# Moving one more chunk's first expert layer to seven block products, and reordering VectorE's work around it

## Chip, cores, metric

One core of a Trainium2 chip (trn2). The metric is the device time of one execution in microseconds (us), the median of several runs. "Span" is the time from the first to the last instruction of the profiled execution; it is 1.7 to 2.1 us shorter than the device time. Runs in a state with a lower granted TensorE clock are marked slow and left out of all comparisons.

## What is computed

The reference, cut to what matters:

```python
# attention: B=4 batches, H=8 heads, S=768, D=64; k and v are mixed over 8 blocks by a
# doubly normalised matrix P (5 rounds of exp and normalising), then attention within blocks
k_sorted = einsum('bhij,bhjcd->bhicd', P, k_blocks)      # v_sorted likewise
attn = softmax(q_block @ k_sorted_block.T / sqrt(D))
x = (attn @ v_sorted_block) -> [3072 tokens, 512]
# expert layer: 4 experts, 512 -> 1024 -> 512
p = domain_probs / (domain_probs.sum(-1) + 1e-9)
for e in range(4):
    h = maximum(x @ w1[e], 0)
    out += p[:, e:e+1] * (h @ w2[e])
```

Almost all matrix work is in the two expert layers, 3072 x 512 x 1024 x 4 twice. The kernel multiplies 2 x 2 blocks of matrices with seven block products instead of eight, at the price of sums of blocks before and after. The second layer does so for all experts at once in nearly all chunks; the first layer only in some.

## The kernel before

The tokens go through in twelve chunks of 256, three to a batch; I number them 0 to 11. While TensorE works on the chunks of batch *b*, the attention of batch *b+1* is laid between its products at numbered "slots" by a plan of entries (chunk, slot, function, batch, pair):

```python
PLANS = {0: [ ...
    (2, 2, st_lk, 2, 1), (2, 2, st_bk, 2, 1), (2, 3, st_a, 1, 2),      # st_bk: pattern for the K mix
    (2, 4, st_x, 1, 2), (2, 4, st_q, 2, 0), (2, 5, st_s, 1, 3),
    (2, 5, st_q, 2, 1), (2, 6, st_v, 2, 0), (2, 7, st_a, 1, 3), ...    # st_v: V mix, st_s: scores, st_a: attention
```

First layer with all products (chunks 0 to 5): 32 matmuls of 256 columns to an expert, each half evacuated by VectorE (taken out of its PSUM bank, with relu and weighting, and written to `Hb`), then sums of blocks of the result for the second layer:

```python
def chunk_first(b, c, es, first, slot):
    for e in es:
        for g in range(2):
            # 4 x 4 matmuls into two PSUM banks ... (cut)
            nc.vector.scalar_tensor_tensor(out=Hb[:, e, ...], in0=ps[:], scalar=0.0, op0=ALU.max,
                                           in1=pb[...], op1=ALU.mult)
            if e > first:
                for w in ((1,), (2,) if b or c else (2, 3))[g]:
                    h_sums(e - 1, w)
            slot()
```

First layer with seven products (chunks 6 to 11): 7 x 8 matmuls of 128 columns to an expert. Products 1, 6, 7, 4 run through one bank X (1 is made in Z and copied), 5 and 3 through a bank Q; ScalarE copies between them and VectorE finishes the quarters:

```python
def p1(): product(Z, "a11", "b11", True); nc.scalar.copy(X, Z)
def p5(): product(Q, "s1", "t1", True)
def p6(): product(X, "s2", "t2");         nc.scalar.copy(u2, X)
def p2(): product(Z, "a12", "b21");       finish(0, 0, Z)
def p7(): product(X, "s3", "t3");         nc.scalar.copy(u3, X); tt(t22, Q, u3, ALU.add)
def p4(): product(X, "a22", "t4");        finish(1, 0, X)
def p3(): product(Q, "s4", "b22");        tt(t12, Q, u2, ALU.add)
```

It needs four sums of weight blocks to an expert (s1 to s4, 128 x 1024 each). Before the change VectorE makes all sixteen, nearly all of them during chunk 5. The results of matmuls go to eight PSUM banks: the kernel uses four for chunk and second layer (psM), four for attention (psA). Attention is over in chunk 5, and `last_banks` hands first psA, later psM to the seven-product scheme.

The softmax here doesn't subtract the row's maximum and nothing guards it: scores larger than these inputs give would overflow.

Of the kernel before, what the change touches and what calls it, by code (L numbers as in the profile page):

```python
# [17 lines left out]
def kernel(  # L18
# [411 lines left out]
    def st_a(b, pr):  # L430
        if b == B - 1 and pr >= H // 2 - 2:
            xsl = arena[:, ds((pr + 2) * NB * 2 * D, NB * 2 * D)].rearrange("p (i h d) -> p i h d", i=NB, h=2)[0:BLK]
        else:
            xsl = att.tile([P, NB, 2, D], F16, name=f"xsl_{b}_{pr}", tag="xsl")[0:BLK]
        xsls[(b, pr)] = xsl
        vs = vss[(b, pr // 2)]
        for hh in range(2):
            ET = ETs[2 * (pr % 2) + hh]
            ps = psa([P, 2, 512], F32, f"ps_a_{b}_{pr}_{hh}")
            for i in range(NB):  # L440
                nc.tensor.matmul(  # L441
                    ps[:, i // HB, ds((i % HB) * VW, D + 1)],
                    ET[:, ds(i * BLK, P)],
                    vs[:, i, 2 * (pr % 2) + hh, 0:D + 1],
                    start=True, stop=True,
                )
            normalize(ps, xsl, hh)
# [153 lines left out]
    def st_bk(b, qd):  # L601
# [6 lines left out]
            (0, 9, st_v, 1, 0), (0, 10, st_q, 1, 0), (0, 10, st_v, 1, 1), (0, 11, st_k, 1, 0), (0, 11, st_n, 1, 1),  # L608
# [6 lines left out]
            (2, 1, st_n, 2, 2), (2, 1, st_n, 2, 3), (2, 2, st_lk, 2, 1), (2, 2, st_bk, 2, 1), (2, 3, st_a, 1, 2),  # L615
            (2, 4, st_x, 1, 2), (2, 4, st_q, 2, 0), (2, 5, st_s, 1, 3),
            (2, 5, st_q, 2, 1), (2, 6, st_v, 2, 0), (2, 7, st_a, 1, 3), (2, 8, st_x, 1, 3), (2, 8, st_v, 2, 1),
# [3 lines left out]
            (0, 0, st_k, 2, 1), (0, 1, st_lk, 3, 0), (0, 1, st_n, 3, 1), (0, 2, st_a, 2, 0), (0, 2, st_q, 2, 3),  # L621
# [112 lines left out]
    def h_sums(e, which):  # L734
        blk = lambda kh, tok: Hb[:, e, ds(kh * KH, KH), ds(tok * P, P)]
        sm = [Sb[:, n, e].rearrange("p (f x) -> p f x", f=KH) for n in range(4)]
        tt = nc.vector.tensor_tensor
        if which == 1:
            tt(sm[0], blk(0, 1), blk(1, 1), ALU.add)  # L739
        elif which == 2:  # L740
            tt(sm[1], sm[0], blk(0, 0), ALU.subtract)
        elif which == 3:
            tt(sm[2], blk(0, 0), blk(0, 1), ALU.subtract)
        else:
            tt(sm[3], blk(1, 0), sm[1], ALU.subtract)
# [13 lines left out]
    def chunk_first(b, c, es, first, slot):  # L759

        xT = xTs[b].rearrange("p k i x -> p k (i x)")
        pb = pbs[(b, c)]
        for e in es:
            for g in range(2):
                ps = psm([P, 4, 2 * P], F32, f"ps_h_{b}_{c}_{e}_{g}")
                for f in range(4):
                    for kc in range(NKC):
                        nc.tensor.matmul(  # L768
                            ps[:, f, :],
                            w1sb[e][:, kc, ds((4 * g + f) * P, P)],  # L770
                            xT[:, kc, ds(2 * c * P, 2 * P)],
                            start=(kc == 0), stop=(kc == NKC - 1),
                        )
                nc.vector.scalar_tensor_tensor(  # L774
                    out=Hb[:, e, ds(4 * g, 4), :], in0=ps[:], scalar=0.0,
                    op0=ALU.max, in1=pb[:, ds(e, 1), :].broadcast_to([P, 4, 2 * P]), op1=ALU.mult,
                )
                if e > first:
                    for w in ((1,), (2,) if b or c else (2, 3))[g]:
                        h_sums(e - 1, w)  # L780
                slot()

    def chunk(b, c, slot, done=()):
# [5 lines left out]
        for w in range(1, 3 if b else 1 + c if c else 3):  # L789
            h_sums(E - 1, w)  # L790
# [6 lines left out]
        def product(n, lhs, rhs, pool=psm):  # L797
            ps = pool([P, DH], F32, f"ps_{n}_{b}_{c}")
            for e in es:
                if pool is last_bank and e == 2:  # L800
                    last["e0"][6]()
# [19 lines left out]
        if b or c:  # L821
            two = [psm([P, 2, 512], F32, f"ps_p{n}_{b}_{c}") for n in range(2)]
            bankA, bankB, bankC, bankQ = [two[n // 2][:, n % 2, 0:DH] for n in range(4)]
            if last:
                bankQ = last["Q"][1][:, 0:DH]
        if b:
# [9 lines left out]
            for e in es:  # L836
                h_sums(e, 3)
# [3 lines left out]
            for e in es:  # L841
                h_sums(e, 4)
# [3 lines left out]
            times(bankA, sm(2), "t3", es, False)  # L846
# [4 lines left out]
            times(bankQ, sm(3), "b22", es, False, True, last["e0"][6] if last else None, 2 if last else None)  # L851
# [4 lines left out]
        if c:  # L856
# [7 lines left out]
            for w in range(1 + c, 3):  # L864
                h_sums(E - 1, w)
# [81 lines left out]
    def a_block(n):  # L947
        return arena[:, ds(n * AW, AW)].rearrange("p (k f) -> p k f", k=2)


    A_ORDER = (6, 7, 8, 0, 1, 2, 3, 4, 5, 9, 10, 11)
    As = []
    for e in range(E):
# [4 lines left out]
            "s1": a_block(A_ORDER[3 * e]), "s3": a_block(A_ORDER[3 * e + 1]), "s2": a_block(A_ORDER[3 * e + 2]),  # L958
        })

    def input_sums(e, n, half=None):
        a = As[e]
        dst, x, y, op = (
            ("s1", "a21", "a22", ALU.add), ("s3", "a11", "a21", ALU.subtract),
            ("s2", "s1", "a11", ALU.subtract), ("s4", "a12", "s2", ALU.subtract),
        )[n]
        part = slice(None) if half is None else slice(half, half + 1)
        nc.vector.tensor_tensor(a[dst][:, part], a[x][:, part], a[y][:, part], op)
# [3 lines left out]
    G0 = 2 * (R // 2)  # L972
    GN = B * (R // 2)

    def token_sums(g):
# [7 lines left out]
            "t1": t3[:, 0], "t2": t3[:, 1], "t3": t3[:, 2],  # L983
            "t4": wide[g % 2][:, 0:2 * P].rearrange("p (k x) -> p k x", k=2),
        }
        for dst, x, y in (("t1", "b12", "b11"), ("t2", "b22", "t1"), ("t3", "b22", "b12"), ("t4", "b21", "t2")):
            nc.vector.tensor_tensor(t[dst], t[x], t[y], ALU.subtract)
# [14 lines left out]
    def prepare_last():  # L1002

        last_banks(0)
        last["n"] = 1
        t = moe.tile([P, NKC, NB, BLK], F16, name="tmp7", tag="xT").rearrange("p k i x -> p (k i x)").bitcast(F32)
        room = [t[:, ds(n * 512, 512)] for n in range(3)]
        for m in range(2):
            t = att.tile([P, NB, 4, VW], F16, name=f"tmp7_{m}", tag="vs").rearrange("p i h w -> p (i h w)")
            t = t[:, 0:2048].bitcast(F32)  # L1010
            room += [t[:, 0:512], t[:, 512:1024]]
        t = att.tile([P, NB, 2, D], F16, name="tmp7_2", tag="xsl").rearrange("p i h d -> p (i h d)").bitcast(F32)
        room.append(t)
        for n, nm in enumerate(("u2", "u3", "t22", "t12")):
            last[nm] = room[2 * n:2 * n + 2]

    def last_bank(shape, dtype, name):
        n = last["n"]
        last["n"] += 1
        return last["Q"][2 - n % 2][:, 0:shape[1]]  # L1020

    def seven(g, e):

        a, t, pb = As[e], Bs[g], pbs[divmod(g, R // 2)]
        X, Z, u2, u3, t22, t12 = [last[nm][e % 2] for nm in ("X", "Z", "u2", "u3", "t22", "t12")]
        X, Z, Q = X[:], Z[:], last["Q"][e][:]
# [30 lines left out]
        def p6():  # L1057
            product(X, "s2", "t2")
# [29 lines left out]
    def last_chunk(g):  # L1088
        b, c = divmod(g, R // 2)
        final = g == GN - 1  # L1090
        last["e0"][2]()
        if g == G0:
            last_banks(1)
        prs = [last["e0"]] + [seven(g, e) for e in range(1, E)]
        for e in range(1, E):
# [3 lines left out]
            if e > 1:  # L1099
                prs[e - 2][12]()  # L1100
            now[5]()
# [5 lines left out]
            for n in late_sums.pop((g, e), ()):  # L1107
                input_sums(*n)
# [5 lines left out]
        bankB, bankA, bankC, bankQ = [t[:, 0:DH] for t in last["Q"]]  # L1114
# [35 lines left out]
        for e in range(E):  # L1150
            h_sums(e, 4)
# [4 lines left out]
        for e in range(E):  # L1156
            h_sums(e, 3)
        product(bankQ, sm(3), "b22", False, range(2))
        if not final:
            token_sums(g + 1)  # L1160
        product(bankA, sm(2), "t3", False)
        if not final:
            last_begin(g + 1)
# [3 lines left out]
        product(bankQ, sm(3), "b22", False, range(2, E), None if final else last["e0"][6], 3)  # L1167
# [8 lines left out]
        (1, 11, 0, 0), (1, 13, 0, 1), (2, 1, 0, 2), (2, 3, 1, 0), (2, 5, 1, 1), (2, 7, 1, 2),  # L1176
        (2, 8, 2, 0), (2, 9, 2, 1), (2, 10, 2, 2), (2, 10, 0, 3), (2, 11, 1, 3), (2, 11, 3, 0), (2, 12, 2, 3),
        (2, 13, 3, 1), (2, 14, 3, 2),
    ]
    late_sums = {(G0, 1): [(3, 3, 0)], (G0, 2): [(3, 3, 1)]}  # L1180
# [112 lines left out]
    for b in range(2):  # L1293
        for c in range(R // 2):
            done = (1, 2) if (b, c) == (0, 0) else ()
            at = [2 * len(done)]

            def slot(b=b, c=c, at=at):
                here = (c, at[0])
                for cc, n, f, *args in PLANS[b]:  # L1300
                    if (cc, n) == here:
                        f(*args)
                if b:
                    for cc, n, e, m in PLAN_A:
                        if (cc, n) == here:
                            input_sums(e, m)
                    if here == (R // 2 - 1, 7):
                        prepare_last()
                    if here == (R // 2 - 1, 12):
                        token_sums(G0)  # L1310
                    if here == (R // 2 - 1, 13):
                        last_begin(G0)
                at[0] += 1

            chunk(b, c, slot, done)
    for g in range(G0, GN):
# [29 lines left out]
```

## Time and profile before

| | before |
|---|---|
| device time, median of 6 runs | 365.28 us (364.46 to 365.92) |
| span of the profiled run | 362.5 us, clock 1.000 |
| chunk 1, 2, 3, 4 (start to start of TensorE's first product) | 23.05, 24.64, 32.20, 32.94 us |
| chunk 5 (to expert 0's second product of chunk 6, both dummy matmuls counted in) | 28.02 us |
| chunks 7 to 11 | 24.7 us each |

The busy time by engine, from the page of the kernel before (us, share of the span, instructions; PEld is the loading of weights, beside PE):

```profile
PE 354.1 (98%) x4517; PEld 314.6 (87%) x4517; DVE 280.0 (77%) x559; ACT 157.7 (44%) x282; POOL 117.5 (32%) x134
```

How to read what follows. In TensorE's order of time each line is a group of matmuls: start, printed length, source line, output<-inputs, shape, count. Printed lengths run into the next group, so lengths are taken from start to start. "Landing" is the time from the issue of a transfer to its arrival. A bracket at the end of a line names how long the engine was idle before it and what released it. Source lines differ by a few between kernels: L1032 before is L1038 after, L1121 is L1141.

### The profile page before, as it was taken

How to read it: one execution, taken by the hardware profiler on the slowest of the kernel's cores; microseconds unless marked ns; L12 is line 12 of the kernel's file. 1: busy time of each engine (PE TensorE's matmuls, PEld its weight loads, DVE VectorE, ACT ScalarE, POOL GpSimd, SP SyncE). 2: the span in 40 equal slices, each digit the busy share in tenths (PEclk: the TensorE clock that was granted, in tenths of full speed). 3: DMA queues.
4: the chain of work that ended last, by engine and by line, in shares of the span. 5: the costliest groups of instructions: out<-in, count | busy, mean ns of one | idle time of the engine just before them, and what ended most of it. 6: DMA issues, size and time to landing. Idle time of an engine off the chain costs nothing.

```text
span 362.5 us, 10556 instructions
## 1 busy us (share of the span) xinstructions
PE 354.1 (98%) x4517; PEld 314.6 (87%) x4517; DVE 280.0 (77%) x559; ACT 157.7 (44%) x282; POOL 117.5 (32%) x134
## 2 busy tenths in 40 slices
PE   8799999999999999999999999999999999999996
PEld 8685857888888888988888899999999998999995
DVE  5753898779798676866799979868779679587794
ACT  2664430452424355367400157165283381561740
POOL 8882011655022420000000018137055082180470
PEclk9999999999999999999999999999999999999999
DMA  8999999999999999934450310310301101102101
GB/s 109 206 208 230 208 210 200 194 186 158 175 197 162 210 91 172 161 85 73 85 126 2 58 60 4 58 60 4 88 31 49 71 2 60 61 2 65 55 16 44
DMA packets 69753, 38.34 MB, mean 106 GB/s; under 512 B 40390, under 2 KB 64716, under 8 KB 69708
## 3 DMA queue, kind: packets, MB, share of 16 engines
q0 software_dynamic: 34640, 17.83, 38.5%
q1 hardware_dynamic: 35068, 19.85, 27.0%
q8 instruction: 35, 0.57, 0.6%
q14 instruction: 10, 0.08, 0.1%
HBM read 42.00 MB, written 6.34 MB: 133 GB/s over the span
## 4 chain that ended last, share of the span: by engine, by line
PE 86%; DVE 6%; DMA 5%; issue 1%; ACT 1%; POOL 1%; DVEq 0%; ACTq 0%
PE ps_Q L1121 20%; PE ps_h L768 18%; PE ps_p L753 13%; PE ps_X L1032 9%; PE ps_Z L1032 6%; PE ps_Q L1032 6%; DMA w<-in_moe_w_dram 4%; PE ps_o L696 3%; PE ps_p L803 2%; PE ps_h L661 1%; PE ps_s L406 1%; PE ps_a L441 1%; PE ps_k L387 1%; DVE Hb L774 1%; PE ps_v L354 1%
## 5 line engine op out<-in xcount | busy, mean ns | idle before, releaser
L1045 POOL TENSOR_TENSOR Hb<-tmp,pb 128x512 f16<-128x512 f32 x48 | 62.0, 1297 | 150.5 <-ACT tmp L1044 148.7
L768 PE MATMUL ps_h<-xT,w 128*128 128x256 f16 x672 | 78.4, 273 | 0.0
L768 PEld LDWEIGHTS <-w 128*128 128x128 f16 x672 | 64.5, 98 | 8.5
L774 DVE SCALAR_TENSOR_TENSOR Hb<-ps_h,pb 128x1024 f16<-128x1024 f32 x42 | 51.3, 1223 | 17.6 <-PE ps_h L768 17.4
L1032 PEld LDWEIGHTS <-w 128*128 128x128 f16 x768 | 46.6, 98 | 0.8
L1121 PEld LDWEIGHTS <-Sb 128*128 128x128 f16 x384 | 37.2, 98 | 4.1
L1032 PEld LDWEIGHTS <-arena 128*128 128x128 f16 x576 | 34.7, 98 | 0.1
L1044 ACT ACTIVATE tmp<-tmp 128x512 f32<-128x512 f32 x48 | 30.5, 635 | 6.4 <-DVE tmp L1076 5.2
L753 PEld LDWEIGHTS <-Sb 128*128 128x128 f16 x288 | 27.4, 98 | 4.2 <-issue 0.7
L1121 PEld LDWEIGHTS <-Hb 128*128 128x128 f16 x288 | 27.4, 98 | 2.9
L413 ACT ACTIVATE ET<-ps_s 96x768 f16<-96x768 f32 x24 | 18.1, 802 | 26.1 <-PE ps_s L406 25.8
L1032 PE MATMUL ps_X<-kT,arena 128*128 128x128 f16 x384 | 29.3, 219 | 0.0
L121 POOL DMA_DIRECT2D arena<-in_q_dram x24 | 19.9, 837 | 27.1 <-DMA qT<-arena 17.2
L396 ACT CAST kT<-ps_k 64x384 f16<-64x384 f32 x48 | 22.7, 473 | 13.2 <-PE ps_k L387 12.2
L739 DVE TENSOR_TENSOR Sb<-Hb 128x512 f16<-128x512 f16 x45 | 26.5, 609 | 0.0
L1068 DVE TENSOR_TENSOR tmp<-ps_Q,tmp 128x512 f32<-128x512 f32 x24 | 16.6, 691 | 12.2 <-ACT tmp L1067 8.0
L1121 PE MATMUL ps_Q<-w,Sb 128*128 128x256 f16 x192 | 24.7, 273 | 0.0
L1121 PE MATMUL ps_Q<-w,Hb 128*128 128x256 f16 x192 | 23.9, 273 | 0.0
L1052 ACT COPY ps_X<-ps_Z 128x512 f32<-128x512 f32 x24 | 13.7, 570 | 22.8 <-PE ps_Z L1032 22.4
L753 PEld LDWEIGHTS <-Hb 128*128 128x128 f16 x216 | 20.6, 98 | 3.1 <-issue 0.3
L1121 PE MATMUL ps_Q<-T,Sb 128*128 128x256 f16 x192 | 22.9, 273 | 0.0
L1059 ACT COPY tmp<-ps_X 128x512 f32<-128x512 f32 x24 | 14.1, 586 | 12.2 <-PE ps_X L1032 12.2
(189 smaller groups left out, 605.3 us busy)
## 6 DMA issues: line engine op xcount, KB each, us to landing
w<-in_moe_w_dram POOLq DMA_DIRECT2D x7, 1024.0 KB, 27.0
pb<-p_dram SPq DMA_DIRECT2D x12, 512.0 KB, 5.5
arena<-in_k_dram POOLq DMA_DIRECT2D x8, 384.0 KB, 8.6
arena<-in_v_dram POOLq DMA_DIRECT2D x8, 384.0 KB, 9.6
vs<-arena SPq DMA_DIRECT2D x36, 66.0 KB, 5.2
arena<-in_q_dram POOLq DMA_DIRECT2D x24, 96.0 KB, 6.7
out_dram<-ob SPq DMA_DIRECT2D x9, 256.0 KB, 2.0
out_dram<-oa SPq DMA_DIRECT2D x8, 256.0 KB, 2.4
```

Source lines behind the costliest of these rows:

```text
L121: nc.gpsimd.dma_start(t[:, h // 2, :, h % 2, :], q[b, h].rearrange("(t p) d -> p t d", p=P))
L396: nc.scalar.copy(kT[ds(D * hh, D), r], pk[ds(D * r, D), hh].rearrange("p a (i c) -> p a i c", c=CP),)
L413: nc.scalar.activation(ETs[2 * (pr % 2) + hh][:, 0:S].rearrange("c (a x) -> c a x", a=2), pss[hh][0:BLK, :, 0:HS], AF.Exp, bias=0.0, scale ...
L739: tt(sm[0], blk(0, 1), blk(1, 1), ALU.add)
L753: nc.tensor.matmul(ps, lhs(e, f), Ts[e][rhs][:, f, :], start=(first and e == es[0] and f == 0), stop=(done and e == es[-1] and f == KH - 1 ...
L768: nc.tensor.matmul(ps[:, f, :], w1sb[e][:, kc, ds((4 * g + f) * P, P)], xT[:, kc, ds(2 * c * P, 2 * P)], start=(kc == 0), stop=(kc == NKC ...
L774: nc.vector.scalar_tensor_tensor(out=Hb[:, e, ds(4 * g, 4), :], in0=ps[:], scalar=0.0, op0=ALU.max, in1=pb[:, ds(e, 1), :].broadcast_to([P ...
L1032: nc.tensor.matmul(dst[:, ds(f * P, P)], a[lhs][:, k, ds(f * P, P)], t[rhs][:, k, :], start=(first and f == 0 and k == 0), stop=(f == KH - ...
L1044: nc.scalar.activation(src, src, AF.Relu, bias=0.0, scale=1.0)
L1045: nc.gpsimd.tensor_tensor(Hb[:, e, ds(i * KH, KH), ds(j * P, P)], src.rearrange("p (f x) -> p f x", f=KH), pb[:, ds(e, 1), ds(j * P, P)].b ...
L1068: tt(t22, Q, u3, ALU.add)
L1121: nc.tensor.matmul(ps, lhs(e, f), Ts[e][rhs][:, f, :], start=(first and e == 0 and f == 0), stop=(e == E - 1 and f == KH - 1), skip_group_ ...
```

## The change

Its intent: chunk 5 takes the cheaper first layer for experts 1 to 3 (expert 0 keeps all products and fills the time of the changeover). For that the weight sums must be ready earlier. Expert 1's stay on VectorE, those of experts 2 and 3 become a scaling on ScalarE and an accumulating transfer issued by GpSimd, expert 0's come during chunk 5. Two block sums of the result are written in place, which frees a quarter of `Sb` twice for other tiles. Around it VectorE's order is changed: the K pattern goes a chunk later, block sums go behind both evacuations ("late"), output adds ahead of one block sum.

```diff
         0: [
-            (2, 1, st_n, 2, 2), ..., (2, 2, st_lk, 2, 1), (2, 2, st_bk, 2, 1), (2, 3, st_a, 1, 2),
+            (2, 1, st_n, 2, 2), ..., (2, 2, st_lk, 2, 1), (2, 3, st_a, 1, 2),
-            (2, 5, st_q, 2, 1), (2, 6, st_v, 2, 0), (2, 7, st_a, 1, 3), (2, 8, st_x, 1, 3), ...
+            (2, 5, st_q, 2, 1), (2, 6, st_a, 1, 3), (2, 7, st_v, 2, 0), (2, 8, st_x, 1, 3), ...
         1: [
-            (0, 0, st_k, 2, 1), (0, 1, st_lk, 3, 0), ...
+            (0, 0, st_k, 2, 1), (0, 0, st_bk, 2, 1), (0, 1, st_lk, 3, 0), ...
@@ chunk_first
-                if e > first:
-                    for w in ((1,), (2,) if b or c else (2, 3))[g]:
+                late = e == E - 1 or b > c
+                if e > first and (g or not late):
+                    two = (2,) if b or c else (2, 3)
+                    for w in (1, *two) if late else ((1,), two)[g]:
                         h_sums(e - 1, w)
@@ chunk: the last expert's second block sum, chunk 2
-        for w in range(1, 3 if b else 1 + c if c else 3):
+        for w in range(1, 2 if c and not b else 3):
             h_sums(E - 1, w)
             ...
             tt(oa1, bankB, oa1, ALU.add)
-            for w in range(1 + c, 3):
-                h_sums(E - 1, w)
+            h_sums(E - 1, 2)
@@ input_sums
+        if vector:
+            nc.vector.tensor_tensor(a[dst], a[y], a[x], ALU.add if sign > 0 else ALU.subtract)
+        else:
+            nc.scalar.mul(a[dst], a[x], sign)
+            nc.gpsimd.dma_start(a[dst], a[y], accum_op=ALU.add)
@@ last_chunk (lead: chunk 5)
+        if lead:
+            chunk_first(b, c, [0], 0, slot)
+            last_banks(0)
+            last_tmp(g)
+            prs = {1: seven(g, 1)}
+            prs[1][1]()
+            prs[1][5]()
+            seven(g, 2)[5]()
+            prs[1][2]()
+            prs[1][6]()
+            input_sums(0, 0, True)
+            input_sums(0, 1, True)
+            last_banks(1)
@@
     PLAN_A = [
+        (1, 8, 1, 0, True), (1, 8, 1, 1, True), (1, 8, 1, 2, True), (1, 10, 1, 3, True),
+        (1, 8, 2, 0), (1, 8, 2, 1), (1, 9, 3, 0), (1, 10, 3, 1), (1, 11, 2, 2), (1, 12, 3, 2), (1, 13, 2, 3),
+        (2, 0, 3, 3),
     ]
   (cut: in-place block sums, homes of tiles, signs of sums, temporaries, the loop over chunks,
    an earlier query transpose at (0, 7))
```

## The prediction

> **What bounds the kernel now.** I read the clock and the 40-slice table first, then the chain of work that ended last, then TensorE's own order of time beside VectorE's, chunk by chunk. A chunk is 256 tokens: a first expert layer with relu and weighting, then a second layer as one matrix product with seven block products. There are twelve, three to a batch; I number them 0 to 11.
>
> The 40-slice table:
>
> ```profile
> PE   8799999999999999999999999999999999999996
> DVE  5753898779798676866799979868779679587794
> PEclk9999999999999999999999999999999999999999
> ```
>
> The clock is full throughout and TensorE is 90% busy or more from the fourth slice on. Busy TensorE is not TensorE without waits, so the next thing to read is where its groups start. The chain, around the chunk that the change rewrites (chunk 5) and in a later chunk:
>
> ```profile
> 183.82 14.03 PE ps_h L768 x128
> 198.07 3.49 PE ps_p L753 x32
> 201.56 1.75 PE ps_Q L753 x16
> ...
> 238.99 0.89 PE ps_X L1032 x16
> ```
>
> From these come two rates. Wide matmuls (256 columns, L768 and L753) take 1.75/16 = 109 ns each, narrow ones (128 columns, L1032) 0.89/16 = 55.6 ns. I use 109.1 and 55.6. A later chunk has 4 experts x 56 narrow and 112 wide: 12.46 + 12.22 = 24.7 us. The busy table by stretch shows that such a chunk really takes that:
>
> ```profile
> 183.66:212.13 28.47, 28.47 (x280) 25.46 (x277) 26.57 (x51) 2.65 (x6) 0.00 (x0) 1.00 0.27 57
> 236.88:261.60 24.72, 24.72 (x339) 23.45 (x337) 19.42 (x41) 12.74 (x25) 10.32 (x8) 1.00 0.18 45
> ```
>
> (Columns: stretch, its length, then busy PE, weight load, DVE, ACT, POOL.) So from chunk 6 to the tail nothing but TensorE's own work counts, and in chunk 5 too: 240 wide at 109.1 ns, 32 narrow at 55.6 and two dummy matmuls give 28.4 of its 28.47 us. There only removed matmuls pay.
>
> Chunks 1 to 4 also carry the attention of the next batches, and there TensorE waits in places. TensorE's order of time in chunk 2:
>
> ```profile
> 102.24 3.66 PE L768 MATMUL ps_h<-xT,w 128*128 128x256 f16 x32
> 105.83 0.51 PE L406 MATMUL ps_s<-qT,kT 64*128 64x96 f16 x16
> 106.69 1.47 PE L753 MATMUL ps_p<-w,Hb 128*128 128x256 f16 x12 [0.34 <-DVE Hb L774]
> ...
> 111.86 0.49 PE L354 MATMUL ps_v<-arena 128*128 128x384 f16 x2
> 112.67 1.47 PE L753 MATMUL ps_p<-T,Sb 128*128 128x256 f16 x12 [0.32 <-DVE room L863]
> ```
>
> A printed length includes the overlapped end of the last matmul, so I go by starts. Scores (16 matmuls) occupy 0.45 us, a V mix 0.33. Hence 105.83 + 0.45 = 106.28 and the next group starts at 106.69: 0.41 lost. 111.86 + 0.33 = 112.19 against 112.67: 0.48 lost. A third gap of 0.17 lies before 115.35. Chunk 2 loses 1.06 us in all, and both large gaps name VectorE. Its order of time says why:
>
> ```profile
> 101.69 0.69 DVE L327 TENSOR_TENSOR arena<-maskk,Rs 128x512 f16<-128x512 f16 x1
> 102.29 1.22 DVE L774 SCALAR_TENSOR_TENSOR Hb<-ps_h,pb 128x1024 f16<-128x1024 f32 x1
> ...
> 105.42 1.21 DVE L774 SCALAR_TENSOR_TENSOR Hb<-ps_h,pb 128x1024 f16<-128x1024 f32 x1
> ```
>
> A pattern for the K mix (0.60 us to the next start) stands ahead of an evacuation, everything after it is pushed back, and the bank for the second layer comes free at 106.6. Chunk 3 has one gap of the same kind, 126.33 to 126.74 (0.41), behind an attention normalisation; chunk 4 one of 0.27 at 183.4.
>
> **What the Trainium skill says.** "TensorE: Matmul & The Clock Gate", section "Wait — 56ns, not 53.3ns?", gives the warm gap as columns / 2.4 GHz plus about 2.5 ns: 55.6 ns for 128 columns, by its form 109.2 for 256. The trace agrees to 0.1 ns, so halving the columns does not quite halve the time. "Perfetto Trace Analysis", section "Identifying the Most-Contended Engine", warns that matmul busy time is a poor measure of headroom; here too, since 98% is shown with gaps inside. "SBUF — State Buffer", section "Who interferes with whom": a VectorE instruction with two SBUF inputs contends with a GpSimd instruction that reads SBUF. Agreed: the block sum of L739 takes 772 ns in chunk 7, where GpSimd multiplies, and 420 in chunk 5, where it is idle. "DMA: Bandwidth & Descriptors", section "SWDGE vs HWDGE vs iDMA", lets only GpSimd issue an accumulating transfer; no transfer of this kernel accumulates, so its cost cannot be read here.
>
> **The change, part by part.**
>
> 1. *Chunk 5, experts 1 to 3, first layer by seven products.* Removed: 3 x 32 wide = 3 x 3.49 = 10.47 us. Added: 3 x 56 narrow = 3 x 3.11 = 9.34 us. All lie on the path: **-1.13 us**. The entry to the scheme moves from chunk 5's end to its beginning and has less to hide behind: expert 1's products have only one or two others between them (0.45 us each), while a copy on ScalarE takes 0.57 to 0.59 and must end before the bank is added to or reused. I expect two or three waits of 0.1 to 0.2 us, plus some delay because VectorE now does two weight sums of expert 0 there (2 x 0.60): **+0.5 us**.
>
> 2. *Weight sums.* Sixteen VectorE sums of 1024 columns (0.60 start to start, four of them split) become eight on VectorE and eight made of a ScalarE scaling plus an accumulating transfer. VectorE is freed of some 4.8 us; TensorE does not wait for those now, so this alone is **0**. The scalings cost ScalarE about 1.0 us each (from 0.57 for 512 and 0.80 for 768 columns, an estimate), 8 us in chunk 4's second half, where it is under half busy. I laid them between its present work: the softmax exponentials at 174.5 and 179.1 slip by about 0.2 us, and their users start 1 us later. The transfers move 256 KB; plain ones of that size land in 2.0 to 6.8 us. First use comes about 15 us after issue. Hidden.
>
> 3. *Chunk 2.* The K pattern leaves the path ahead of the evacuations (-0.60 of VectorE), the first block sum of the last expert goes behind its second evacuation (-0.33), one attention product goes a slot earlier, and one block sum goes behind two output adds. Shifting VectorE's list gives the first evacuation's end near 106.2, before TensorE's 106.28, and the adds at 110.1 instead of 111.75. The gaps of 0.41, 0.48 and 0.17 close; the moved product may wait about 0.2 for its exponential, which ends at 107.94: **-0.85 us**.
>
> 4. *Chunk 3.* The pattern now sits in an idle 0.86 us of VectorE; block sums go behind evacuations, which brings the normalisation at 125.77 forward by 0.33: **-0.33 us** of the 0.41 gap.
>
> 5. *In-place block sums, output sums ahead, homes of the tiles, the earlier query transpose.* Same instructions at the same cost; they free room. **0**.
>
> Sum: -1.13 + 0.5 - 0.85 - 0.33 = -1.8 us, from the median of 365.67: **363.8 us**.
>
> **The rivals.** (a) *VectorE becomes the bound in chunk 5.* A seven-product expert gives it 4 passes of 0.60, and there are block sums, token sums and four weight sums besides. It is 19.4 busy in a later chunk; less one expert's 2.4, plus two evacuations (2.4), four weight sums (2.4) and the tail of the attention (1.8) makes about 23.6 of 25.1 us. Before, it carried 26.57 of 28.47 without stopping TensorE, which speaks against; but the extra work comes at the start, where banks are scarce. It would eat the whole 1.13: 365. (b) *Accumulating transfers are slow or hold GpSimd*, whose multiplications chunk 5 now needs. The chain of three per expert would have to take over 5 us a link to matter. If so, TensorE stops for 1 to 3 us: 366 to 368. (c) *The gaps of chunk 2 move rather than close*, for the second layer reuses four banks in turn and the exponential ends late: the gain there is 0.2 and the time 364.5. (d) *All of it works without entry waits*: 363.2.
>
> **Range and chances.** The three runs of before spread over 1.2 us, and rivals (a) and (c) are likelier than a windfall, so the range goes further up: 362.4 to 365.5. A gain over 2% needs 7.3 us, and the whole disputed work is 1.13 us of matmuls and some 1.7 us of gaps; a loss over 2% needs a new wait of 7 us. Faster 0.01, same 0.97, slower 0.02.
>
> **What would show it.** Chunk 5's first layer should hold 32 wide matmuls and 168 narrow ones more; from its start to the first second-layer product of chunk 6 the time should fall by 0.6 to 1.1 us. Chunk 2 should shrink from 24.64 to about 23.8, chunk 3 from 32.20 to 31.9, chunk 4 stay at 32.9 within 0.3, and chunks 7 to 11 stay at 24.7. A TensorE wait on an accumulating transfer, on GpSimd or on ScalarE's scalings, or chunk 4 longer by over 0.5 us, would prove me wrong.

## The result

| | before | changed |
|---|---|---|
| device time, median of 6 | 365.28 us | 362.98 us (362.52 to 364.18) |
| ratio | | 0.9944, 95% interval 0.9921 to 0.9967 |
| span of the profiled run | 362.5 us | 362.4 us |

A ratio is the mean time of one kernel's fast runs over that of the other's in the same rounds, so it is not quite the ratio of the two medians. Here it means 2.0 us less (0.56% of 365.3; the interval is 1.2 to 2.9 us): the same by the 2% rule, clear of noise by the interval, and within 1 us of the 363.8 predicted. A second measurement in a later round of runs (the control below) gave 0.9947, 1.9 us less.

The profiled run of the changed kernel was its slowest (364.18), so its span hides the gain. The waits of TensorE in that run (us in total, times, longest) begin with the reason:

```profile
PE ps_s L406 <- DMA qT<-arena: 1.9, 1, 1.9
```

The first scores of batch 1, in chunk 1, waited 1.9 us for a transposed query. The run of before has no such wait, and neither has the control run of the changed kernel, whose span is 361.3 us. With start-to-start times one can still read every chunk by itself:

| us | chunk 1 | chunk 2 | chunk 3 | chunk 4 | chunk 5 |
|---|---|---|---|---|---|
| before | 23.05 | 24.64 | 32.20 | 32.94 | 28.02 |
| changed, first profile | 25.16 | 23.94 | 32.00 | 33.15 | 27.40 |
| changed, control | 23.20 | 23.94 | 31.87 | 33.15 | 27.40 |
| control less before | +0.15 | -0.70 | -0.33 | +0.21 | -0.62 |

After chunk 5 the control takes 150.67 us and before 150.82, another -0.15. The sum is -1.44 us.

A further 0.3 us lies outside the spans. Device time less span is 2.01 to 2.14 us in every fast run of the kernels without the new chunk 5 (before, e1, e2, e3, e7) and 1.72 to 1.90 in every fast run of those with it; in the rounds of the control the means are 2.06 and 1.75. The mean spans there differ by 1.57 us (363.05 and 361.48), close to the sum of the stretches. What makes the 0.3 us no trace shows.

Busy time by engine, from the changed kernel's page. TensorE has more, shorter matmuls and the same busy time; VectorE has 3 us less, ScalarE and GpSimd 16 and 17 us more:

```profile
PE 354.0 (98%) x4589; PEld 315.0 (87%) x4589; DVE 276.8 (76%) x560; ACT 173.6 (48%) x305; POOL 134.1 (37%) x148
```

The busy table of the changed kernel by stretch, chunk 5 and a later chunk (stretch, length, PE, PEld, DVE, ACT, POOL):

```profile
184.34:212.19 27.85, 27.78 (x352) 25.60 (x349) 23.40 (x48) 11.26 (x21) 11.03 (x9) 1.00 0.52 99
236.93:261.65 24.72, 24.72 (x339) 23.45 (x337) 18.09 (x41) 12.75 (x24) 10.32 (x8) 1.00 0.19 44
```

Against 28.47 before, chunk 5 is 0.62 shorter; it is not all busy any more, 27.78 of 27.85. The later chunk is what it was. VectorE is not full in chunk 5, at 23.4 of 27.85 us.

Chunk 2 in TensorE's order of time, changed kernel:

```profile
107.20 0.51 PE L406 MATMUL ps_s<-qT,kT 64*128 64x96 f16 x16
107.73 1.47 PE L753 MATMUL ps_p<-w,Hb 128*128 128x256 f16 x12
109.04 0.74 PE L441 MATMUL ps_a<-vs,ET 96*128 96x65 f16 x16
109.62 1.48 PE L753 MATMUL ps_p<-w,Hb 128*128 128x256 f16 x12
...
113.00 0.49 PE L354 MATMUL ps_v<-arena 128*128 128x384 f16 x2
113.32 1.47 PE L753 MATMUL ps_p<-T,Sb 128*128 128x256 f16 x12
...
114.97 1.04 PE L753 MATMUL ps_p<-T,Hb 128*128 128x256 f16 x8
116.02 1.47 PE L753 MATMUL ps_p<-T,Sb 128*128 128x256 f16 x12
```

107.20 + 0.45 = 107.65, and the second layer starts at 107.73: the gap of 0.41 has become 0.08. The one of 0.48, behind the V mix, is closed: 113.00 + 0.33 = 113.33. The attention product takes 0.58 instead of 0.49, a short wait for its exponential. One gap stands as before: 114.97 + 0.87 = 115.84 against 116.02. VectorE beside it:

```profile
103.32 1.23 DVE L774 SCALAR_TENSOR_TENSOR Hb<-ps_h,pb 128x1024 f16<-128x1024 f32 x1 [0.19 <-PE ps_h L768]
...
106.47 2.34 DVE L774 SCALAR_TENSOR_TENSOR Hb<-ps_h,pb 128x1024 f16<-128x1024 f32 x2
...
114.54 1.09 DVE L745 TENSOR_TENSOR Sb<-Hb,Sb 128x512 f16<-128x512 f16 x3
115.55 0.41 DVE L872 TENSOR_TENSOR room<-ps_p,room 128x256 f32<-128x256 f32 x1
```

The evacuation at 103.32 now waits for TensorE and not the other way round, and the last two follow each other directly (x2). The gap that is left has its reason in the last two lines: an output add, which frees the bank, stands behind two rows of three block sums that nobody needs yet.

The gap of chunk 3, first before, then in the control:

```profile
124.58 1.91 PE L768 MATMUL ps_h<-xT,w 128*128 128x256 f16 x16
126.74 0.50 PE L354 MATMUL ps_v<-arena 128*128 128x384 f16 x2 [0.25 <-DVE xsl L423]
```

```profile
124.27 1.91 PE L768 MATMUL ps_h<-xT,w 128*128 128x256 f16 x16
126.10 0.50 PE L354 MATMUL ps_v<-arena 128*128 128x384 f16 x2
```

Sixteen matmuls take 1.75 us, so 0.41 us were lost before and 0.08 are lost now.

The entry into the seven products in chunk 5 of the changed kernel, TensorE (expert 1's and 2's products of 0.445 us each):

```profile
190.50 0.61 PE L1038 MATMUL ps_Z<-xT,w 128*128 128x128 f16 x8
191.17 0.61 PE L1038 MATMUL ps_X<-kT,arena 128*128 128x128 f16 x8
191.76 0.61 PE L1038 MATMUL ps_Z<-xT,w 128*128 128x128 f16 x8
```

and ScalarE:

```profile
190.53 0.59 ACT L1065 COPY tmp<-ps_X 128x512 f32<-128x512 f32 x1 [1.23 <-PE ps_X L1038]
191.14 0.57 ACT L1058 COPY ps_X<-ps_Z 128x512 f32<-128x512 f32 x1
```

190.50 + 0.445 = 190.95, but the product into X starts at 191.17, when the copy out of X has just ended; the next, into Z, waits for the second copy. With two later gaps of 0.08 the entry costs 0.22 + 0.14 + 0.08 + 0.08 = 0.52 us. The later two pass through VectorE: expert 1's third product (193.18) waits for an addition that itself began only when ScalarE's next copy ended (192.41), and before 195.05 a copy stands behind an evacuation.

The accumulating transfers of the changed kernel (instructions on GpSimd: least, median, longest ns, first and last start; then the landing of the transfers):

```profile
L969 POOL DMA_DIRECT2D arena<-w x4: 1203/1371/1784, 172.6 to 177.9; - x4
...
DMA to landing us min/median/max: 4.8/5.7/7.3
```

### The profile page after: what moved, and what is told of

It is laid out like the page before. It is cut to its first block, busy times and chain, and to the rows that moved or that the text cites. A ratio compares the mean times of both kernels' runs of the same rounds, so it can differ in the third digit from the quotient of the medians.

```text
span 362.4 us, 10776 instructions
## 1 busy us (share of the span) xinstructions
PE 354.0 (98%) x4589; PEld 315.0 (87%) x4589; DVE 276.8 (76%) x560; ACT 173.6 (48%) x305; POOL 134.1 (37%) x148
## 4 chain that ended last, share of the span: by engine, by line
PE 75%; DMA 18%; DVE 3%; SPq 1%; ACT 1%; issue 1%; POOL 0%; DVEq 0%; ACTq 0%; POOLq 0%
PE ps_Q L1141 24%; PE ps_h L768 13%; PE ps_p L753 10%; PE ps_X L1038 10%; DMA arena<-in_q_dram 8%; PE ps_Q L1038 7%; PE ps_Z L1038 7%; DMA w<-in_moe_w_dram 6%; DMA vs<-arena 2%; DMA qT<-arena 2%; PE ps_a L441 2%; PE ps_s L406 1%; SPq L368 1%; PE ps_v L354 1%; PE ps_k L387 1%
## 5 line engine op out<-in xcount | busy, mean ns | idle before, releaser
L1051 POOL TENSOR_TENSOR Hb<-tmp,pb 128x512 f16<-128x512 f32 x40 | 50.8, 1277 | 84.3 <-ACT tmp L1050 83.1
L768 PE MATMUL ps_h<-xT,w 128*128 128x256 f16 x576 | 67.8, 273 | 0.0
L774 DVE SCALAR_TENSOR_TENSOR Hb<-ps_h,pb 128x1024 f16<-128x1024 f32 x36 | 44.0, 1223 | 19.8 <-PE ps_h L768 19.6
L1141 PEld LDWEIGHTS <-Hb 128*128 128x128 f16 x560 | 53.4, 98 | 5.6
L1141 PE MATMUL ps_Q<-w,Hb 128*128 128x256 f16 x336 | 43.4, 273 | 0.0
L1141 PE MATMUL ps_Q<-T,Hb 128*128 128x256 f16 x224 | 26.7, 273 | 0.0
L1050 ACT ACTIVATE tmp<-tmp 128x512 f32<-128x512 f32 x40 | 25.4, 634 | 1.2 <-DVE tmp L1074 1.0
L753 PEld LDWEIGHTS <-Hb 128*128 128x128 f16 x232 | 21.9, 98 | 3.0
L1141 PEld LDWEIGHTS <-Sb 128*128 128x128 f16 x224 | 21.9, 98 | 2.5
L1051 POOL TENSOR_TENSOR Hb<-tmp7x,pb 128x512 f16<-128x512 f32 x14 | 19.0, 1356 | 5.7 <-ACT tmp7x L1050 5.7
L1044 DVE SCALAR_TENSOR_TENSOR Hb<-ps_X,pb 128x512 f16<-128x512 f32 x27 | 18.5, 684 | 2.7 <-PE ps_X L1038 2.7
```

What stands on the lines that cost most here:

```text
L753: nc.tensor.matmul(ps, lhs(e, f), Ts[e][rhs][:, f, :], start=(first and e == es[0] and f == 0), stop=(done and e == es[-1] and f == KH - 1 ...
L768: nc.tensor.matmul(ps[:, f, :], w1sb[e][:, kc, ds((4 * g + f) * P, P)], xT[:, kc, ds(2 * c * P, 2 * P)], start=(kc == 0), stop=(kc == NKC ...
L774: nc.vector.scalar_tensor_tensor(out=Hb[:, e, ds(4 * g, 4), :], in0=ps[:], scalar=0.0, op0=ALU.max, in1=pb[:, ds(e, 1), :].broadcast_to([P ...
L1044: nc.vector.scalar_tensor_tensor(out=Hb[:, e, ds(i * KH, KH), ds(j * P, P)], in0=src.rearrange("p (f x) -> p f x", f=KH), scalar=0.0, op0= ...
L1050: nc.scalar.activation(src, src, AF.Relu, bias=0.0, scale=1.0)
L1051: nc.gpsimd.tensor_tensor(Hb[:, e, ds(i * KH, KH), ds(j * P, P)], src.rearrange("p (f x) -> p f x", f=KH), pb[:, ds(e, 1), ds(j * P, P)].b ...
```

## The experiments

Chunk lengths of profiled runs. In chunks 2, 4 and 5 kernels with the same code there agree to 0.02 us, so a single profile tells more than the times do, whose medians wander by 0.5 us and more.

| us | 1 | 2 | 3 | 4 | 5 | median | ratio to before, interval |
|---|---|---|---|---|---|---|---|
| e1_pattern | 23.05 | 24.32 | 32.20 | 32.95 | 28.02 | 364.23 | 0.9979 (0.9961 to 0.9998) |
| e2_plan | 23.05 | 24.19 | 32.21 | 32.94 | 28.02 | 364.18 | 0.9979 (0.9965 to 0.9994) |
| e3_all_but_5 | 23.54 | 23.94 | 33.21 | 32.95 | 28.02 | 364.10 | 0.9971 (0.9954 to 0.9988) |
| e4_chunk5 | 23.05 | 24.64 | 32.20 | 33.04 | 27.41 | 363.73 | 0.9974 (0.9945 to 1.0003) |
| e5_vector | 23.20 | 23.95 | 32.78 | 35.77 | 27.41 | 366.24 | 1.0033 (1.0018 to 1.0048) |
| e6_scores | 24.20 | 23.95 | 31.87 | 33.14 | 27.40 | 364.01 | 0.9976 (0.9956 to 0.9997) |
| e7_before_scores | 24.06 | 24.64 | 32.21 | 32.95 | 28.02 | 365.67 | 1.0020 (1.0004 to 1.0036) |
| e8_entry | 23.20 | 23.94 | 31.87 | 33.14 | 28.35 | 364.21 | 0.9978 (0.9961 to 0.9996) |
| e9_best | 23.37 | 23.77 | 31.88 | 33.09 | 28.35 | 364.98 | 1.0003 (0.9980 to 1.0026) |
| e10_after (control) | 23.20 | 23.94 | 31.87 | 33.15 | 27.40 | 363.24 | 0.9947 (0.9930 to 0.9965) |
| e12_three | 23.05 | 23.76 | 33.04 | 33.04 | 26.90 | 362.96 | 0.9933 (0.9896 to 0.9969) |

### e1_pattern, e2_plan: where chunk 2's gain comes from

My theory was that VectorE's list held chunk 2 back; the rival, that its late exponential did. e1 is the kernel before with one entry moved, e2 moves the attention product too.

```diff
-            (2, 2, st_lk, 2, 1), (2, 2, st_bk, 2, 1), (2, 3, st_a, 1, 2),
+            (2, 2, st_lk, 2, 1), (2, 3, st_a, 1, 2),
-            (0, 0, st_k, 2, 1), (0, 1, st_lk, 3, 0),
+            (0, 0, st_k, 2, 1), (0, 0, st_bk, 2, 1), (0, 1, st_lk, 3, 0),
 # e2 as well:
-            (2, 6, st_v, 2, 0), (2, 7, st_a, 1, 3),
+            (2, 6, st_a, 1, 3), (2, 7, st_v, 2, 0),
```

> The kernel before with one edit: the K pattern of 0.60 us goes from chunk 2 to the start of chunk 3. My theory (VectorE's list held chunk 2 back): the gap of 0.41 us before the second layer closes wholly, chunk 2 goes from 24.64 to 24.2 or less, chunk 3 stays at 32.20 within 0.1. Rival (the gaps come from the late exponential or from the block sums): chunk 2 stays at 24.6. Time: 0.4 us less, not to be told from noise.

> The same and the last attention product of batch 1 one slot earlier. Theory: chunk 2 gains a further 0.2 to 0.3, 23.9 to 24.0, for the normalisation no longer stands before the output adds. Rival (it waits for its exponential as long as it saves): no further gain.

Measured: chunk 2 at 24.32 (-0.32) and 24.19 (-0.13 more), chunk 3 unmoved. VectorE's order was the cause, as the theory said, but each step brought a little less than expected. In e1 the gap of 0.41 shrinks to 0.09. In e2 that of 0.48 is gone, but the moved product waits 0.09 and a new gap of 0.24 opens before the V mix; it closes when the block sums move (e3).

### e3_all_but_5, e4_chunk5: the two halves of the change

e3 is e2 with the block sums behind evacuations and the output adds ahead; e4 is the changed kernel with all of that undone.

> All of the change except chunk 5 and what it needs (tile homes, in-place sums): pattern, slot, block sums behind evacuations, output adds ahead of a block sum. Theory: chunk 2 at 23.94 as in the changed kernel, chunk 3 at 32.0, chunks 4 and 5 as before (32.94, 28.0 to 28.1 with the dummy), time 0.9 to 1.1 us less. Rival (chunk 5 is where all the gain lies): time 0 to 0.3 us less.

> The changed kernel with those four schedule edits undone: only chunk 5 by seven products, with its weight sums on ScalarE and by accumulating transfers. Theory: chunks 2 and 3 back at 24.64 and 32.20, chunk 4 at 33.1, chunk 5 at 27.4 instead of 28.0, time 0.3 to 0.6 us less. Rival (the gain is in chunk 5 and the freed VectorE): 1.5 to 2 us less.

Chunk 2 of e3 is 23.94, exactly that of the changed kernel, so the block sums bring the last 0.25. Chunk 5 of e4 is 27.41 against 28.02, chunks 2 and 3 are those of before. Neither half carries the whole: the ratios are 0.9971 and 0.9974, and their savings (0.29% and 0.26%) add up to 0.55%, where the change has 0.56%. e4's interval reaches beyond 1; its profiled run had a clock of 0.991, spent ahead of chunk 1.

Chunk 1 of e3 is 23.54: 0.15 as in the control, and 0.34 because the first scores waited for the query, though the transpose has its old place in e3.

Chunk 3 of e3 came out at 33.21, not 32.0. Among its waits of TensorE stands a new one:

```profile
PE ps_a L441 <- DMA vs<-arena: 1.3, 1, 1.3
```

The attention product of chunk 3 waits for the mixed V that six small transfers spread over partitions. Their landing times, from the view of that tile, in the kernel before:

```profile
L368 SPq DMA_DIRECT2D vs<-arena x6: 573/668/814, 113.2 to 116.8; - x6
...
DMA to landing us min/median/max: 5.1/6.1/6.6
```

in e3:

```profile
L368 SPq DMA_DIRECT2D vs<-arena x6: 573/632/1114, 113.2 to 117.1; - x6
...
DMA to landing us min/median/max: 7.2/7.8/7.9
```

and in the control of the changed kernel, where nothing waits:

```profile
L368 SPq DMA_DIRECT2D vs<-arena x6: 573/606/655, 113.4 to 116.6; - x6
...
DMA to landing us min/median/max: 4.9/5.7/6.0
```

The landing varies from run to run. Before, the V mix (start 111.86) and its user (124.09) were 12.23 us apart; a run of the changed kernel without the wait has 112.02 and 123.78, 11.76. The shortened chunk 2 and 3 took half a microsecond off that slack. In the profiles with chunk 2 at 24.19 or more (before, e1, e2, e4, e7) the wait never shows, not even in e4, where the transfers landed in 6.8 to 7.5 us; in those with 23.76 to 23.95 it shows in four of eight (0.22 in the first profile of the changed kernel, 0.8 in e5, 1.1 in e12, 1.3 here). That is a part of the gain given back in some runs and not in others, which the prediction did not have; what makes the landing vary is not shown. Where there is no such wait, chunk 3 is 31.87, 0.33 under before.

### e5_vector: are the accumulating transfers needed?

```diff
-        (1, 8, 2, 0), (1, 8, 2, 1), (1, 9, 3, 0), (1, 10, 3, 1), (1, 11, 2, 2), (1, 12, 3, 2), (1, 13, 2, 3),
-        (2, 0, 3, 3),
+        (1, 8, 2, 0, True), (1, 8, 2, 1, True), ...  (all eight on VectorE, same slots)
```

> The changed kernel with the eight weight sums of experts 2 and 3 back on VectorE (at the same slots), none by accumulating transfer. Prediction on record: moving them was worth nothing by itself, since TensorE does not wait for them; then chunk 4 stays at 33.15 within 0.2, chunk 5 at 27.4 within 0.2, time equal to the changed kernel's within 0.4. Rival (VectorE has no room for 4.8 us more in the second half of chunk 4): chunk 4 or 5 gets 0.5 to 2 us longer with TensorE waiting on VectorE.

The rival won, and by more than it claimed: chunk 4 is 35.77, 2.62 us longer, and the kernel is slower than before (by 0.33%, clear of noise by the interval, though the 2% rule counts it as the same). The busy table for the second half of chunk 4 (from the second layer's first product; columns as above), in e5:

```profile
167.79:186.74 18.95, 16.67 (x217) 14.13 (x216) 18.42 (x42) 7.57 (x14) 0.00 (x0) 1.00 0.34 78
```

and in the control of the changed kernel:

```profile
166.80:183.23 16.43, 16.32 (x219) 14.15 (x218) 14.93 (x37) 15.02 (x22) 5.75 (x5) 1.00 0.89 148
```

VectorE is full, 18.42 of 18.95 us, where the changed kernel leaves it 1.5 us of air and puts 15.0 us on ScalarE. TensorE's order of time in e5 shows the waits, all on VectorE:

```profile
174.74 0.21 PE L406 MATMUL ps_s<-qT,kT 64*128 64x96 f16 x1 [0.49 <-DVE xsl L423]
175.58 0.51 PE L406 MATMUL ps_s<-qT,kT 64*128 64x96 f16 x15 [0.62 <-DVE xsl L423]
176.51 1.91 PE L753 MATMUL ps_p<-T,Sb 128*128 128x256 f16 x16 [0.42 <-DVE oa L830]
```

Scores need a bank that the normalisation (L423) frees, and the normalisation stands behind weight sums. So the transfers are what makes chunk 5's seven products pay at these slots. Whether VectorE could make the sums at other slots, spread over more chunks, was not tried.

### e6_scores, e7_before_scores: the wait for the query

The first scores one slot later, in the changed kernel and in the kernel before:

```diff
-            (1, 0, st_s, 1, 0), (1, 0, st_n, 1, 2), (1, 1, st_k, 1, 1),
+            (1, 0, st_n, 1, 2), (1, 1, st_s, 1, 0), (1, 1, st_k, 1, 1),
```

> The changed kernel with the first scores of batch 1 one slot (2.1 us) later. The profiled run of the changed kernel, its slowest of six, waited 1.89 us there for a transposed query. If that wait, which depends on when a load lands, makes the spread of its runs (362.5 to 364.2): the runs come to lie within 0.6 us of each other near 362.5, and chunk 1 at 22.9 to 23.1. Rival (the spread has another source): spread and median as before, 363.0.

> The same edit on the kernel before, whose runs lay at 364.5 to 364.9 or at 365.7 to 365.9. If the wait for the query makes the upper group, all runs come to lie near 364.6, and the gain of the change is then 2.0 us between kernels without that wait. Rival: both groups remain.

Both missed. The wait for the query is gone, but the K mix, now right behind the scores, waits for a bank that their exponential holds. The waits of TensorE in e6:

```profile
PE ps_k L387 <- ACT ET L413: 1.0, 1, 1.0
```

Chunk 1 is 24.20 and 24.06: a wait that came now and then was traded for one that stands in both profiles (1.0 us in e6, 0.9 in e7). The spread of e6 (363.3 to 365.9) did not shrink; that of e7 did (365.4 to 366.1), 1 us too high. So the query makes at most a part of the spread, and what makes the rest stays open.

### e8_entry, e9_best: filling the entry, two attempts that failed the same way

The second half of expert 0's first layer laid between expert 1's first products:

```diff
-            chunk_first(b, c, [0], 0, slot)
+            (first half of expert 0, its evacuation, two quarters of the second half)
             last_banks(0)
             ...
             prs[1][1]()
             prs[1][5]()
-            seven(g, 2)[5]()
+            (third quarter)
             prs[1][2]()
             prs[1][6]()
+            (fourth quarter, its evacuation)
 # expert 2's fifth product goes back to its usual place in the loop
 # e8 allots the banks of last_banks(1) in another order, e9 in the changed kernel's;
 # e9 also: K mix and scores of chunk 1 exchanged, output add ahead of block sums
 # in chunks 1 and 2, expert 1's weight sums spread over more slots
```

> The changed kernel with the second half of expert 0's first layer in chunk 5 laid between the first products of expert 1, and expert 2's fifth product back in its usual place. Same matmuls. Theory: the entry waits of the changed kernel (0.22, 0.14, 0.08, 0.08: 0.52 us) shrink to 0.2 or less and chunk 5 goes from 27.40 to 27.0 or 27.1, the time by 0.3 to 0.5. Rival (VectorE, not ScalarE's copies, holds the entry): the waits stay or move, chunk 5 at 27.4 or longer.

> The changed kernel with four edits, each to be read in its own chunk: the scores and the K mix of the first slots of chunk 1 trade places (no wait for the query, and none for the exponential: chunk 1 at 23.05 or below); in chunks 1 and 2 the second row of block sums goes behind an output add (0.17 less in each: chunk 2 at 23.77); in chunk 4 expert 1's sums on VectorE are spread (chunk 4 at 32.98); in chunk 5 the interleaved entry again, now with the banks in the changed kernel's order, so that the products' banks lie on the half that is emptied first (chunk 5 at 26.9 to 27.0 instead of 27.40). Sum: 0.9 us and the query wait less than the changed kernel. Rival: the interleaved entry stalls again at the bank (chunk 5 at 28.3), then VectorE's second evacuation and not the place of the banks held the last attempt.

In both, chunk 5 is 28.35. TensorE at the dummy matmul of the second set of banks, in e8:

```profile
190.39 0.38 PE L1004 MATMUL ps_X<-w 128*128 128x512 f16 x1 [1.31 <-DVE Hb L1108]
```

and in e9:

```profile
189.36 0.38 PE L1004 MATMUL ps_X<-w 128*128 128x512 f16 x1 [1.31 <-DVE Hb L1108]
```

The second evacuation of expert 0, now late, releases the bank, wherever the bank lies in the allotment: I had supposed after e8 that the order of banks was at fault, and e9 refuted it. It looks as if the new set of banks waits for the whole old pool. Apart from this one wait no gap is left in the entry of e8; 27.40 - 0.52 + 1.48 (the hole from 188.91 to 190.39) = 28.36, and 28.35 is measured. The other edits of e9 kept their promise in chunk 2 (23.77) but not in chunk 1 (23.37: the scores, exchanged with the K mix, take 0.76 us instead of 0.45), and its unprofiled runs were slower than the profiled one by up to 2.9 us, for which no profile shows the cause.

### e10_after: the control

> The changed kernel itself once more, as the control for the next one. The stretches that the runs so far fix to 0.02 us (chunk 2: 23.94, chunk 4: 33.15, chunk 5: 27.40) should come out the same; chunk 1 between 23.05 and 25.2 and chunk 3 between 31.87 and 33.2, as the query and the spread V land. Ratio to the kernel before 0.993 to 0.997.

All as expected; its numbers stand in the result.

### e11_entry2, e12_three: filling the entry without touching banks

```diff
             seven(g, 2)[5]()
-            prs[1][2]()
             prs[1][6]()
+            prs[1][2]()
@@ expert 2, after expert 1's seventh product
+            else:
+                (four matmuls of the second layer's first product for expert 0, taken out of their later place)
             now[2]()
 # e12 also: in chunks 1 and 2 output add ahead of the second row of block sums;
 # expert 1's sums at (1, 8), (1, 10), (2, 0), (2, 1)
```

> The changed kernel with its entry reordered without touching the banks: expert 1's sixth product ahead of its second, and expert 0's four matmuls of the second layer's first product as filler before expert 2's second. Same matmuls. If ScalarE's copies are what the entry waits for, the 0.52 us of waits go nearly whole: chunk 5 at 26.9 to 27.0 instead of 27.40, time 0.4 us under the changed kernel's, about 362.8. Rival (other waits take their place, on the sum in SBUF that VectorE makes of the fifth product): chunk 5 at 27.2 or more.

> The same, with two edits of the kernel that ran no faster than before (0.17 us from block sums behind an output add in chunks 1 and 2; expert 1's sums on VectorE spread out, two of them now in chunk 5), without its exchange of scores and K mix. If that exchange made it slow: chunk 2 at 23.77, chunk 4 at 33.0, chunk 5 at 27.0, time 0.7 us under the changed kernel's. Rival (a shorter chunk 2 meets the spread of V later on): chunk 3 at 32.0 to 33.4 by a wait for the spread V, and no gain in time.

e11's five fast runs: 362.1 to 363.6, ratio 0.9935. e12 has the same entry. TensorE there:

```profile
190.71 0.61 PE L1038 MATMUL ps_X<-kT,arena 128*128 128x128 f16 x8
191.16 0.60 PE L1126 MATMUL ps_Q<-w,Hb 128*128 128x256 f16 x4
191.59 0.61 PE L1038 MATMUL ps_Z<-xT,w 128*128 128x128 f16 x8
```

Each group starts where the one before ends, the filler (L1126) included. Chunk 5 is 26.90: the whole 0.5 us of entry waits came from ScalarE's copies with too little beside them. Against before chunk 5 is now 1.12 us shorter, which is the 1.13 of the removed matmuls. Chunk 2 is 23.76 and chunk 4 33.04. But in the profiled run chunk 3 lost it again:

```profile
124.83 0.66 PE L441 MATMUL ps_a<-vs,ET 96*128 96x65 f16 x16 [1.08 <-DMA vs<-arena]
```

By the clock e12's median is 362.96, its ratio 0.9933 (0.9896 to 0.9969), against the changed kernel's 0.9944 and 0.9947. It beats the kernel before. That it beats the changed kernel is shown for chunks 1, 2, 4 and 5 (0.15 + 0.18 + 0.11 + 0.50 = 0.94 us together), and not shown for the time: the wait for the spread V and the wandering of the runs are as large.

## Why the prediction was right, and where it was not

The time was 0.8 us below the number and within the range. The number started from 365.67, the median of three runs; from the 365.28 of six the same -1.8 us gives 363.5. That the sum came so close to the measured -2.0 is in part luck: the parts that were priced came to -1.65 instead of -1.81, and +0.15, +0.21, -0.15 and the 0.3 outside the spans were not foreseen. By its steps:

1. **Chunk 5: right in sum and in its parts.** -0.63 was predicted, -0.62 measured, and the entry waits are 0.52 where 0.5 stood. What makes them was only half right. They start from ScalarE's copies: e12 puts other products beside the copies and no wait is left. VectorE's two weight sums, which the prediction also counted there, hold up nobody: e12 keeps them at their place, and in the changed kernel VectorE was idle for 0.44 us after them, waiting for ScalarE.
2. **Weight sums, "this alone is 0": wrong as a statement of what they are worth.** The step reasoned from the kernel before, where TensorE did not wait for these sums. But there they had all of chunk 5; the change needs them in the second half of chunk 4, where e5 puts the cost of leaving them on VectorE at 2.62 us. The step lacked the question where the sums would have to go. The rest of it held: scalings of 1.05 us (estimated 1.0), transfers landing in 4.8 to 7.3 us, all hidden. Chunk 4 grew by 0.21, within the 0.3 allowed.
3. **Chunk 2: mechanism right, -0.85 was -0.70.** Pattern 0.32, slot 0.13, block sums 0.25 (e1 to e3). The missing 0.15 is a difference: 0.08 of the first gap and the last one of 0.18 stay, and the moved product waits 0.09 instead of 0.2. The prediction closed the last gap by shifting the whole list; it stays since the output add that frees the bank is still behind block sums, and e12 moves it and gains 0.18.
4. **Chunk 3: exactly -0.33 where nothing intervenes, but a new wait was overlooked.** The spread of V had under a microsecond to spare, and the gain of chunks 2 and 3 uses it up; 0.2 to 1.3 us go back in half of the profiles with the shortened chunk 2.
5. **"0" for the rest: nearly.** Chunk 1 became 0.15 longer in kernels with the late block sums (e3 onward; the same output add behind the same block sums, which e12 cures), and the chunks after chunk 5 0.15 shorter, since no weight sums are left in chunk 6.

The fixed stretches thus sum to -1.44 us, the part outside the spans brings -0.3, and the times say -1.9 to -2.0, with intervals of 1.2 to 2.9 and 1.3 to 2.6. What is left lies within the intervals; whether the part before chunk 1, which ended anywhere between 69.97 and 71.26 us in the fast profiles (74.03 in the one with a clock of 0.991) though its products are the same in all of them, has a share, these runs cannot tell. Of the rivals, (a), VectorE as the bound in chunk 5, did not come; it came in chunk 4 as soon as the transfers were taken away. (b), slow transfers, did not come. (c), gaps that move rather than close, came in a small way: in e2 before the V mix, in the changed kernel as the wait for V in chunk 3, while chunk 2's last gap simply stayed.

Four readings of the prediction are off without harm. The slices show TensorE at 90% from the third on, not the fourth, and the last one is at 60%. One weight sum is split in the kernel before, not four (the trace has 15 whole ones and two halves). Chunk 6 was not TensorE's own work alone: it had two gaps of 0.09 us (before 218.03 and 219.90), behind a split weight sum on VectorE; the control has none there. And rival (a) sets 23.6 us of VectorE against 25.1, which leaves out four products and two dummy matmuls that the 28.47 of before includes; by its own rates the stretch is about 27.3 us, and 23.4 of 27.85 were measured, so VectorE was never as near the bound as it feared.

## What to carry to other kernels

When an engine is full, read each stretch from start to start and price a change there: here 0.02 us were readable by stretch while the run times wandered by 1 us. "Nobody waits for this work now" does not say what it will cost at its new place; add up the busy time of the stretch that it must move into. And a stretch made shorter takes slack from every transfer that was issued before it: look up the landing times beside the time to first use before counting the gain.

## What the Trainium skill lacked or had wrong

- "TensorE: Matmul & The Clock Gate", section "Back-to-back issue gap", gives about 81 ns for each matmul of 128 columns in a sustained stream of weight loads and matmuls. Here such a stream runs at 0.445 us for eight, 55.6 ns, each with its own weight load, for some 75 us of the kernel before (24 x 56 of them). The section "Wait — 56ns, not 53.3ns?" of the same page has it right.
- "DMA: Bandwidth & Descriptors", section "SWDGE vs HWDGE vs iDMA", says who may issue an accumulating transfer but has no time for one. Here 128 x 1024 f16 within SBUF took GpSimd 0.86 to 1.78 us to issue and 4.8 us at least, 5.7 in the median and 7.3 at most to land; in the control 4.0, 5.8 and 7.5.
- No page that I used says how much the landing of one and the same small transfer varies. The six of 66 KB that spread V landed in 4.9 to 6.0 us in one run of the changed kernel and 5.8 to 7.0 in another, and in 7.2 to 7.9 in e3.
